# One-core decode block: 32 rows of the query weights by an indirect load in place of two side loads

## The chip, the core and the metric

The kernel runs on one core of one Trainium2 chip. The core has five engines that run their own instruction streams in order: PE (matrix products), DVE (vector), ACT (scalar), POOL (GpSimd) and SP (which here only starts transfers). Sixteen DMA engines move data between the chip's memory (HBM) and the on-chip memory of 128 partitions. The metric is device microseconds (us) of one execution; before the change three runs gave 138.19, 138.13 and 137.70 us, median 138.13 us.

## What is computed

A decode step of a transformer block, for four tokens (B = 4), all tensors in bf16:

```python
def _A_ref(x, k_cache, v_cache, wq, wo):          # attention over the last W = 2048 positions
    q = (x @ wq).reshape(B, 1, 32, 128).transpose(0, 2, 1, 3)
    k = jnp.repeat(k_cache[:, :, Sk - W:, :], rep, axis=1)     # 4 kv heads, rep = 8
    v = jnp.repeat(v_cache[:, :, Sk - W:, :], rep, axis=1)
    scores = jnp.einsum("bhqd,bhkd->bhqk", q, k) * (Dh ** -0.5)
    p = _softmax(scores, axis=-1)
    o = jnp.einsum("bhqk,bhkd->bhqd", p, v)
    return o.transpose(0, 2, 1, 3).reshape(B, 1, 4096) @ wo

def _B_ref(x, w1, w3, w2):                        # gated MLP, F = 3584
    h = _silu(x @ w1) * (x @ w3)
    return h @ w2

h = x + _A_ref(_layernorm(x), k_cache, v_cache, wq, wo)
h2 = h + _B_ref(_layernorm(h), w1, w3, w2)
```

Here x is 4 x 1024, wq 1024 x 4096, wo 4096 x 1024, w1 and w3 1024 x 3584, w2 3584 x 1024. With four tokens the arithmetic is small; 55.6 MB of weights and cache must be read.

## The kernel before

**The ring.** Every large operand is loaded by SP into one on-chip tile, `ring`, 81,920 bf16 columns wide on all 128 partitions (160 KiB each; `KIB` = 512 columns). `plan` (line 129) lists the loads in order with the column at which each lands, and `load_next` (line 149) issues the next entry wherever the code calls it. A region is used again once its earlier content has been read. With columns in brackets: wq rows 0 to 3 of each partition [0, 16384), wq rows 4 to 7 [16384, 32768), K of tokens 0 and 1 [32768, 49152), K of tokens 2 and 3 [49152, 65536), V of tokens 0 and 1 [65536, 81920), that is token 0 in [65536, 73728) and token 1 in [73728, 81920), V of tokens 2 and 3 [0, 16384), wo [16384, 49152), w1 [49152, 77824), w3 [0, 28672), and w2 in four pieces [28672, 57344).

**Who waits.** A framework tracks tiles in the order in which the program text names them: an instruction that reads columns waits for the last instruction named before it that writes them, and one that writes them waits for earlier readers and writers. Each load also waits for the landing of an earlier load whose semaphore it takes over. A planner then sets the order of each engine's instructions; each engine runs its own list strictly in order. SP's list decides when transfers start.

**Stages.**
- Layer norm of x, then `xn` is turned into `xnT` (line 196): partition p holds wq's input rows 8p to 8p + 7, row chunk kc = 8p + kc.
- The query product (lines 255 to 279): for each of 8 chunks kc, eight matmuls of 512 columns add into `q_ps`. Chunks 0 to 3 need the first wq load, chunks 4 to 7 the second.
- In chunk 7 the last 512 columns (`CE`) are not in the second load. They come in two side loads (`load_side`, line 115) into two `kT` buffers, on 20 and 12 partitions, four sets of rows each. Matching parts of `xn` are copied to `xs`, turned to `xsT` (lines 199 to 219), and eight matmuls (line 273) add the product.
- `q_sb`, `qt_ps`, `qz` (lines 280 to 290): the queries scaled, turned and spread.
- The K stage (lines 312 to 332): 16 units (token b, quarter n). Each has 16 PE transposes of K into two `kt_ps` buffers, a DVE copy and an ACT copy into a `kT` buffer, and, one unit later, four score matmuls that need `qz`. There are four `kt_ps` buffers and four `kT` buffers. wo's load is issued after unit 7.
- Softmax and its spreading `z` (lines 335 to 361), then 256 `OT_ps` matmuls with V (lines 380 to 390). w1's load is issued behind those of tokens 0 and 1, whose columns it overwrites.
- wo (lines 409 to 420; w3's and w2's first loads are issued in and behind it), the second layer norm up to `hnT`, w1 and w3 (`gate_up`), w2 (`down`), and the output.

`load_next(7)` at line 159 issues the first seven entries, up to V of tokens 0 and 1; line 271 issues V of tokens 2 and 3 behind chunk 3.

Of the kernel before, what the change touches and what calls it, by code (L numbers as in the profile page):

```python
# [10 lines left out]
P = 128  # L11
ACT = mybir.ActivationFunctionType
ALU = mybir.AluOpType
AX = mybir.AxisListType
BF16 = mybir.dt.bfloat16
FP32 = mybir.dt.float32


@with_exitstack
def kernel(  # L20
# [13 lines left out]
    nc = tc.nc  # L34

    B, _, D = A_x.shape
# [5 lines left out]
    KC = D // P  # L42
# [15 lines left out]
    ktpool = ctx.enter_context(tc.tile_pool(name="ktpool", bufs=4))  # L58
    wide = ctx.enter_context(tc.tile_pool(name="wide", bufs=2))
    const = ctx.enter_context(tc.tile_pool(name="const", bufs=1))  # L60
    act = ctx.enter_context(tc.tile_pool(name="act", bufs=1))
# [3 lines left out]
    JG = 4  # L65
    QD = P // JG
    RS = QD // B
    CQ = Hq * Dh // JG
# [11 lines left out]
    RING = 5 * 16384  # L80
# [8 lines left out]
    ring = stream.tile([P, RING], BF16)  # L89
# [19 lines left out]
    N_Q, N_F = Hq * Dh, F  # L109


    CE = 512
    SETS = [(0, 5, 4), (80, 3, 4)]

    def load_side(r0, ne, ns):

        t = ktpool.tile([P, JG * QD * 16], BF16, tag="kT")
        rows = A_wq[r0 * KC : (r0 + ne * 4 * ns) * KC, N_Q - CE : N_Q]
        rows = rows.rearrange("(t i k) n -> k i t n", i=ne, k=KC)[KC - 1]
        nc.sync.dma_start(out=t[: ne * 4, : ns * CE], in_=rows)  # L120
        return [t[: ne * 4, k * CE : (k + 1) * CE] for k in range(ns)]

    def load_tail(at, src, n, r0, m):

        t = ring[:, at : at + m * n]
        nc.sync.dma_start(out=t[:, : m * n - CE], in_=src[:, r0 * n : (r0 + m) * n - CE])
        return [t[:, k * n : (k + 1) * n] for k in range(m)]
    KIB = 512
    plan = [
        ("wq", load_rows, (0, wq_v, N_Q, 0, 4)),  # L130
        ("side", load_side, SETS[0]),
        ("side", load_side, SETS[1]),
        ("wq", load_tail, (32 * KIB, wq_v, N_Q, 4, 4)),
        ("k", load_kv, (64 * KIB, A_k_cache, 0)),
        ("k", load_kv, (96 * KIB, A_k_cache, 2)),
# [10 lines left out]
    loaded = {}  # L146
    cursor = [0]

    def load_next(n=1):
        for _ in range(n):  # L150
            if cursor[0] < len(plan):
                kind, f, args = plan[cursor[0]]
                loaded.setdefault(kind, []).extend(f(*args))
                cursor[0] += 1

    x_sb = act.tile([B, D], BF16)
    for c in range(2):
        nc.scalar.dma_start(out=x_sb[:, c * 512 : (c + 1) * 512], in_=x_flat[:, c * 512 : (c + 1) * 512])
    load_next(7)

    ident = const.tile([P, P], BF16)
    make_identity(nc, ident[:])
    eps_t = const.tile([P, 1], FP32)
    nc.vector.memset(eps_t[:], eps)

# [2 lines left out]
    for c in range(2):  # L168
        nc.sync.dma_start(
            out=x_q[c * 2 * QD : (c + 1) * 2 * QD : RS, :],  # L170
            in_=x_flat.rearrange("b (j c) -> j b c", j=JG)[2 * c : 2 * c + 2],
        )

    psA_cm = tc.tile_pool(name="psA", bufs=1, space=bass.MemoryType.PSUM)
    psA = psA_cm.__enter__()


    stats = act.tile([B, 2, nc.vector.BN_STATS_DIM], FP32)
    for c in range(2):
        nc.vector.bn_stats(out=stats[:, c, :], in_=x_sb[:, c * 512 : (c + 1) * 512])  # L180
    mv = act.tile([B, nc.vector.BN_AGGR_DIM], FP32)
    nc.vector.bn_aggr(out=mv[:], in_=stats[:])
    rstd = act.tile([B, 1], FP32)
    nc.scalar.activation(out=rstd[:], in_=mv[:, 1:2], func=ACT.Sqrt, bias=eps_t[:B], scale=1.0)
    nc.vector.reciprocal(out=rstd[:], in_=rstd[:])
    xn = act.tile([B, D], BF16)
    nc.vector.tensor_scalar(  # L187
        out=xn[:], in0=x_sb[:], scalar1=mv[:, 0:1], scalar2=rstd[:, 0:1],
        op0=ALU.subtract, op1=ALU.mult,
# [5 lines left out]
    xnT = act.tile([P, KC, B], BF16)  # L195
    nc.vector.tensor_copy(out=xnT[:], in_=tp_ps[:])


    NS = sum(ns for _, _, ns in SETS)
    ts_ps = psA.tile([P, NS, B], BF16, tag="kt1")  # L200
    xs = wide.tile([B, NS, 20], BF16, tag="w4k")
    sl = []
    for r0, ne, ns in SETS:
        v = xn[:, r0 * KC : (r0 + ne * 4 * ns) * KC]
        v = v.rearrange("b (s l i k) -> b k l i s", s=4, l=ns, i=ne)
        nc.vector.tensor_copy(
            out=xs[:, len(sl) : len(sl) + ns, : ne * 4].rearrange("b l (i s) -> b l i s", s=4),
            in_=v[:, KC - 1, :, :, :],
        )
        for l in range(ns):  # L210
            nc.tensor.transpose(
                out=ts_ps[: ne * 4, len(sl), :], in_=xs[:, len(sl), : ne * 4], identity=ident[:B, :B]
            )
            sl.append(ne * 4)
    xsT = act.tile([20, NS, B], BF16)
    k0 = 0
    for _, ne, ns in SETS:
        nc.vector.tensor_copy(out=xsT[: ne * 4, k0 : k0 + ns, :], in_=ts_ps[: ne * 4, k0 : k0 + ns, :])
        k0 += ns


    q_ps = psA.tile([P, CQ], FP32, tag="scores")
    nc.vector.memset(q_ps[:], 0.0)

    qz = act.tile([P, B, Hkv * QD + REP], BF16)
    nc.vector.memset(qz[:], 0.0)
    ident_f = const.tile([P, P], FP32)
    nc.vector.tensor_copy(out=ident_f[:], in_=ident[:])
# [3 lines left out]
        out=perm[:].rearrange("p (h dq) -> p h dq", dq=JG),  # L232
        in_=ident[:].rearrange("p (dq h) -> p h dq", dq=JG),
# [12 lines left out]
    for j in range(2, JG):  # L246
        nc.vector.tensor_tensor(
            out=same[:, 0, :], in0=same[:, 0, :], in1=ident[:, j * QD : (j + 1) * QD], op=ALU.add
# [3 lines left out]
        nc.vector.tensor_copy(out=same[:, j, :], in_=same[:, 0, :])  # L252


    for kc in range(KC):
        wq_t = loaded["wq"][kc]
        for hf in range(CQ // 512):
            for g in range(JG):
                c0 = g * CQ + hf * 512
                n = min(512, N_Q - CE - c0) if kc == KC - 1 else 512  # L260
                if n <= 0:
                    continue
                nc.tensor.matmul(  # L263
                    q_ps[QD * g : QD * g + B, hf * 512 : hf * 512 + n],
                    lhsT=xnT[:, kc, :],
                    rhs=wq_t[:, c0 : c0 + n],
                    start=(kc == 0),
                    stop=(kc == KC - 1 or (kc == KC - 2 and c0 + 512 == N_Q)),
                )
        if kc == RQ - 1:  # L270
            load_next()
            for k, np_ in enumerate(sl):
                nc.tensor.matmul(
                    q_ps[QD * (JG - 1) : QD * (JG - 1) + B, CQ - CE : CQ],
                    lhsT=xsT[:np_, k, :],
                    rhs=loaded["side"][k],
                    start=False,
                    stop=False,
                )
    q_sb = act.tile([P, CQ], BF16)  # L280
    nc.vector.tensor_single_scalar(out=q_sb[:, :512], in_=q_ps[:, :512], scalar=qscale, op=ALU.mult)
    nc.scalar.mul(out=q_sb[:, 512:], in_=q_ps[:, 512:], mul=qscale)
# [1 line left out]
    for r in range(REP):  # L284
        nc.tensor.transpose(out=qt_ps[:, r, :], in_=q_sb[:, r * Dh : (r + 1) * Dh], identity=ident[:])
    nc.vector.tensor_copy(
        out=qz[:, :, : Hkv * QD].rearrange("p b (g z) -> p b g z", g=Hkv)[:, :, :, :REP],
        in_=qt_ps[:].rearrange("p r (g x) -> p x g r", g=Hkv)[:, :B, :, :],
# [24 lines left out]
    for u, (b, n) in enumerate(units):  # L313
        k_v = loaded["k"][b]
        kT = ktpool.tile([P, NJ, P], BF16, tag="kT")
        for t in range(NJ // TB):
            kt_ps = psA.tile([P, TB, P], BF16, tag=f"kt{nt % 4}")
            for jj in range(TB):
                nc.tensor.transpose(  # L319
                    out=kt_ps[:, jj, :], in_=k_v[:, n * NJ + t * TB + jj, :], identity=ident[:]  # L320
# [21 lines left out]
        out=Pm[:], in_=scores_ps[:], func=ACT.Exp, bias=nmax[:], scale=1.0, accum_out=rsum[:]  # L342
# [6 lines left out]
    for c in range(NSB):  # L349
# [4 lines left out]
        for g in range(Hkv):  # L354
            if g % 2 == 0:
                nc.vector.tensor_scalar(  # L356
                    out=z[:, :, g, :], in0=pt_ps[:], scalar1=mask[:, g : g + 1], scalar2=None, op0=ALU.mult
# [10 lines left out]
        out=Dm[:], in0=ident[:].rearrange("p (g b r) -> p b g r", g=Hkv, b=B),  # L368
        scalar1=rinv[:, 0:1], scalar2=None, op0=ALU.mult,
# [10 lines left out]
    for b in range(B):  # L380
        for j in range(JK):
            nc.tensor.matmul(  # L382
                OT_ps[:, b, :],
                lhsT=loaded["v"][b][:, j, :],
                rhs=PTz[j // NJ][:, (j % NJ) * B + b, :, :],
                start=(j == 0),
                stop=(j == JK - 1),
# [21 lines left out]
    for i in range(IO):  # L409
        for j in range(JG):  # L410
            nc.tensor.matmul(  # L411
                y_ps[QD * j : QD * (j + 1), :],
                lhsT=o4[:, i, :, :].rearrange("p b s -> p (b s)"),
                rhs=loaded["wo"][i][:, j * CG : (j + 1) * CG],
                start=(i == 0),
                stop=(i == IO - 1),
# [27 lines left out]
        out=hn[:], in0=h1[:], scalar1=tot[:, 0:1], scalar2=rstd2[:, 0:1],  # L444
        op0=ALU.subtract, op1=ALU.mult,
# [4 lines left out]
        out=hnT[:].rearrange("p k x -> p (k x)"), in_=hn[:].rearrange("q (c k) -> q k c", k=KC)  # L450
# [3 lines left out]
    def gate_up(kind, out_ps):  # L454
# [27 lines left out]
        out=hgT[:].rearrange("p i x -> p (i x)"),  # L482
        in_=hg[:].rearrange("q s c -> q (s c)").rearrange("q (c i) -> q i c", i=IF),
# [18 lines left out]
    for i in range(R1, IF):  # L502
        for c, t in enumerate((ya_ps, yb_ps)):
            down(i, HC, c * HC, t, start=(i == R1), stop=(i == IF - 1), skip_group_check=True)
        if i == R2 - 1:
            for c, t in enumerate((ya_ps, yb_ps)):
                nc.tensor.matmul(
                    t[:, :HC], lhsT=ident_f[:], rhs=h2[:, c * HC : (c + 1) * HC],
                    start=False, stop=False, skip_group_check=True,
# [36 lines left out]
```

## Time and profile before

| quantity | value |
|---|---|
| runs | 137.70 to 138.19 us, median 138.13 us |
| span of the profiled execution | 136.0 us |
| PE, DVE, ACT, POOL busy | 72.3, 43.9, 31.0, 1.7 us |
| data moved by DMA | 55.75 MB, mean 410 GB/s |
| mean granted TensorE clock | 0.720 of full |
| K stage with the scores: first `kt_ps` on the chain to last score matmul | 29.27 to 58.59 us |

The span runs from the first to the last instruction of one profiled execution; the 138.13 us of the runs is 2.1 us more, for what lies around the span. A transfer has two times: its issue on SP, and its landing, when an engine that waits for it goes on. An engine's line "waited for: total, times, longest" says what ended its idle time.

### The profile page before, as it was taken

Reading aid. Unit: us, or ns where it says so; the run is one execution under the profiler, and the core shown is the slowest. Engines: PE = TensorE matmul, PEld = TensorE weight load, DVE = VectorE, ACT = ScalarE, POOL = GpSimd, SP = SyncE. Lnnn points to the kernel's source line nnn. Section 1 sums busy time; section 2 is a strip of 40 time slices with the busy share of each in tenths; the row PEclk is TensorE's granted clock in tenths of the full one; section 3 lists DMA queues with packets and bytes.
Section 4 is the critical chain, followed back from the end, with each engine's and each line's share of the span. In section 5 each row is a group of like instructions: output and inputs, shape, how many; then the busy total and the mean of one; then the engine's idle time right before and its main releaser. Section 6 shows DMA issues by size and latency. Waiting matters only on the chain.

```text
span 136.0 us, 2436 instructions
## 1 busy us (share of the span) xinstructions
PE 72.3 (53%) x1096; PEld 46.1 (34%) x1096; DVE 43.9 (32%) x79; ACT 31.0 (23%) x36; POOL 1.7 (1%) x8
## 2 busy tenths in 40 slices
PE   0004920979898989810525916791097000970981
PEld 0002300268374756500014905570043000430870
DVE  5055000043344444470994001206200596026010
ACT  3000000015555555609294300000001400000000
POOL 5000000000000000000000000000000000000000
PEclk9999975557999999985555555568556855568568
DMA  5999999999999999999989999989989899999970
GB/s 155 464 463 406 412 420 414 429 424 439 424 439 424 424 443 426 410 552 453 463 347 463 463 410 405 477 354 494 439 371 494 371 472 401 399 420 407 424 298 5
DMA packets 2650, 55.75 MB, mean 410 GB/s; under 512 B 296, under 2 KB 464, under 8 KB 720
## 3 DMA queue, kind: packets, MB, share of 16 engines
q1 hardware_dynamic: 2604, 55.58, 95.6%
q8 instruction: 8, 0.13, 0.3%
q10 hardware_dynamic: 36, 0.02, 0.0%
q14 instruction: 2, 0.02, 0.0%
HBM read 55.59 MB, written 0.01 MB: 409 GB/s over the span
## 4 chain that ended last, share of the span: by engine, by line
DMA 54%; PE 25%; ACT 11%; DVE 5%; SPq 2%; issue 1%; ACTq 0%
DMA ring<-in_B_w_dram 38%; DMA ring<-in_A_wq_dram 15%; PE kt_ps L319 11%; ACT kT L325 5%; PE scores_ps L304 5%; ACT z L360 3%; PE q_ps L263 3%; DVE rmax L336 2%; ACT Pm L341 2%; PE OT_ps L382 2%; DVE pT L350 1%; SPq L120 1%; PE g_ps L459 1%; DVE z L356 1%; ACT L341 1%
## 5 line engine op out<-in xcount | busy, mean ns | idle before, releaser
L325 ACT COPY kT<-kt_ps 128x1024 bf16<-128x1024 bf16 x16 | 15.9, 1013 | 13.4 <-PE kt_ps L319 13.4
L319 PE MATMUL kt_ps<-ident,ring 128*128 128x128 bf16 x256 | 18.0, 232 | 0.0
L319 PEld LDWEIGHTS <-ring 128*128 128x128 bf16 x256 | 16.0, 105 | 4.9 <-issue 4.9
L323 DVE COPY kT<-kt_ps 128x1024 bf16<-128x1024 bf16 x16 | 11.1, 692 | 16.5 <-PE kt_ps L319 16.5
L459 PEld LDWEIGHTS <-hnT 128*32 128x32 bf16 x128 | 5.5, 143 | 21.8 <-issue 19.2
L382 PE MATMUL OT_ps<-z,ring 128*128 128x32 bf16 x256 | 7.5, 188 | 8.5 <-ACT z L360 5.0
L459 PE MATMUL u_ps<-ring,hnT 128*32 128x448 bf16 x64 | 6.0, 563 | 11.0 <-DMA ring<-in_B_w_dram 11.0
L304 PE MATMUL scores_ps<-kT,qz 128*32 128x512 bf16 x64 | 9.9, 609 | 2.9 <-ACT kT L325 2.9
L263 PE MATMUL q_ps<-ring,xnT 128*4 128x512 bf16 x63 | 6.7, 595 | 7.8 <-DMA ring<-in_A_wq_dram 7.8
L382 PEld LDWEIGHTS <-ring 128*128 128x128 bf16 x256 | 7.4, 104 | 9.2 <-issue 9.2
L459 PE MATMUL g_ps<-ring,hnT 128*32 128x448 bf16 x64 | 5.9, 558 | 4.9 <-DMA ring<-in_B_w_dram 4.9
L492 PEld LDWEIGHTS <-hgT 128*32 128x32 bf16 x156 | 4.9, 134 | 6.2 <-issue 5.7
L411 PE MATMUL y_ps<-ring,o 128*32 128x256 bf16 x128 | 5.9, 371 | 0.8 <-DVE o L398 0.8
L514 ACT CAST res<-yb_ps 128x128 bf16<-128x128 f32 x1 | 0.3, 266 | 26.1 <-PE yb_ps L492 26.1
L492 PE MATMUL y_ps<-ring,hgT 128*32 128x256 bf16 x68 | 3.8, 419 | 4.4 <-DMA ring<-in_B_w_dram 4.4
L360 ACT ACTIVATE z<-pt_ps,mask 128x512 bf16<-128x512 f32 x8 | 5.3, 687 | 3.5 <-DVE z L356 3.5
L352 PE MATMUL pt_ps<-pT,perm 128*128 128x512 bf16 x4 | 2.4, 607 | 6.8 <-DVE pT L350 6.8
L263 PEld LDWEIGHTS <-xnT 128*4 128x4 bf16 x63 | 2.0, 115 | 11.7 <-issue 11.6
L194 PE MATMUL tp_ps<-ident,xn 4*128 4x4 bf16 x8 | 0.7, 200 | 10.0 <-DVE xn L187 10.0
L356 DVE TENSOR_SCALAR z<-pt_ps,mask 128x512 bf16<-128x512 f32 x8 | 5.5, 741 | 1.2 <-ACT z L360 0.8
L473 DVE RECIPROCAL eg<-eg 128x896 f32<-128x896 f32 x1 | 5.8, 5753 | 0.0
L411 PEld LDWEIGHTS <-o 128*32 128x32 bf16 x128 | 4.4, 131 | 3.1 <-DVE o L398 1.9
(85 smaller groups left out, 50.1 us busy)
## 6 DMA issues: line engine op xcount, KB each, us to landing
ring<-in_B_w_dram SPq DMA_DIRECT2D x2, 7168.0 KB, 22.5
ring<-in_A_k_cache_dram SPq DMA_DIRECT2D x4, 2048.0 KB, 27.6
ring<-in_A_v_cache_dram SPq DMA_DIRECT2D x4, 2048.0 KB, 29.2
ring<-in_B_w_dram SPq DMA_DIRECT2D x1, 4352.0 KB
ring<-in_A_wq_dram SPq DMA_DIRECT2D x1, 4096.0 KB, 12.2
ring<-in_A_wq_dram SPq DMA_DIRECT2D x1, 3968.0 KB
ring<-in_B_w_dram SPq DMA_DIRECT2D x1, 1792.0 KB
ring<-in_B_w_dram SPq DMA_DIRECT2D x1, 768.0 KB
```

The costliest lines, as they stand in the source:

```text
L263: nc.tensor.matmul(q_ps[QD * g : QD * g + B, hf * 512 : hf * 512 + n], lhsT=xnT[:, kc, :], rhs=wq_t[:, c0 : c0 + n], start=(kc == 0), stop ...
L304: nc.tensor.matmul(scores_ps[QD * g : QD * (g + 1), n * 512 : (n + 1) * 512], lhsT=qz_v[:, z0 : z0 + QD], rhs=kT_v[:, g, :, :], start=(b = ...
L319: nc.tensor.transpose(out=kt_ps[:, jj, :], in_=k_v[:, n * NJ + t * TB + jj, :], identity=ident[:])
L323: nc.vector.tensor_copy(out=kT[:, t * TB : (t + 1) * TB, :], in_=kt_ps[:])
L325: nc.scalar.copy(out=kT[:, t * TB : (t + 1) * TB, :], in_=kt_ps[:])
L356: nc.vector.tensor_scalar(out=z[:, :, g, :], in0=pt_ps[:], scalar1=mask[:, g : g + 1], scalar2=None, op0=ALU.mult)
L360: nc.scalar.mul(out=z[:, :, g, :], in_=pt_ps[:], mul=mask[:, g : g + 1])
L382: nc.tensor.matmul(OT_ps[:, b, :], lhsT=loaded["v"][b][:, j, :], rhs=PTz[j // NJ][:, (j % NJ) * B + b, :, :], start=(j == 0), stop=(j == J ...
L411: nc.tensor.matmul(y_ps[QD * j : QD * (j + 1), :], lhsT=o4[:, i, :, :].rearrange("p b s -> p (b s)"), rhs=loaded["wo"][i][:, j * CG : (j + ...
L459: nc.tensor.matmul(out_ps[QD * j : QD * (j + 1), hf, :HF], lhsT=hnT[:, k, :], rhs=loaded[kind][k][:, c0 : c0 + HF], start=(k == 0), stop=( ...
L473: nc.vector.reciprocal(out=eg[:], in_=eg[:])
L492: nc.tensor.matmul(out_ps[QD * j : QD * (j + 1), :n], lhsT=hgT[:, i, :], rhs=loaded["w2"][i][:, j * CG + c0 : j * CG + c0 + n], **kw,)
```

## The change

Chunk 7's part of wq for partitions 96 to 127 (32 whole rows of 4096 columns) leaves the second wq load. That load becomes two: partitions 0 to 95 with four rows, partitions 96 to 127 with three. The 32 rows come by one indirect load from GpSimd into `xg`, the last 4096 columns of the ring [77824, 81920). It has one index for each of 128 partitions; 96 of them are out of bounds and skipped, and `LANES` says which partitions get a row. `xg` is zeroed first by a DVE memset. `sel`, a 0/1 matrix, is built on POOL from nine pieces of `ident`; one matmul with it gives the indices, and another moves the 32 partitions' `xn` to the places where their rows land (`xgT`). Eight matmuls with `xgT` and `xg` are added behind chunk 6, over the whole 4096 columns; chunk 7 then runs on 96 partitions. The side loads, their copies, transposes and matmuls go.

`load_next(7)` becomes `load_next(4)` (wq, wq's rest, both K entries), and one `load_next()` (V of tokens 0 and 1) stands behind the indirect load and ahead of the product with `xg` in the program text.

```diff
-    CE = 512
-    SETS = [(0, 5, 4), (80, 3, 4)]
-    def load_side(r0, ne, ns):
...
+    XP = 96
+    LANES = [(0, 5), (1, 5), (2, 5), (3, 2), (4, 5), (6, 1), (8, 1), (10, 3), (15, 5)]
     def load_tail(at, src, n, r0, m):
         t = ring[:, at : at + m * n]
-        nc.sync.dma_start(out=t[:, : m * n - CE], in_=src[:, r0 * n : (r0 + m) * n - CE])
+        nc.sync.dma_start(out=t[:XP, :], in_=src[:XP, r0 * n : (r0 + m) * n])
+        nc.sync.dma_start(out=t[XP:, : (m - 1) * n], in_=src[XP:, r0 * n : (r0 + m - 1) * n])
...
-        ("side", load_side, SETS[0]),
-        ("side", load_side, SETS[1]),
...
-    load_next(7)
+    load_next(4)
+
+    xg = ring[:, RING - N_Q :]
+    nc.vector.memset(xg, 0.0)
...
+    sel = wide.tile([P, P], BF16, tag="w4k")
+    nc.gpsimd.memset(sel[:], 0.0)
+    m0 = XP
+    for e, n in LANES:
+        nc.gpsimd.tensor_copy(out=sel[:, e * 8 : e * 8 + n], in_=ident[:, m0 : m0 + n])
+        m0 += n
+    pidx = const.tile([P, 1], I32)
+    nc.gpsimd.iota(pidx[:], pattern=[[0, 1]], base=0, channel_multiplier=1)
...
+    pv = const.tile([P, 2], BF16)
+    nc.vector.tensor_copy(out=pv[:, 0:1], in_=pidx[:])
+    nc.vector.memset(pv[:, 1:2], 1.0)
+    id_ps = psA.tile([P, 2], FP32, tag="kt3")
+    nc.tensor.matmul(id_ps[:], lhsT=sel[:], rhs=pv[:], start=True, stop=True)
...
+    nc.vector.tensor_tensor(out=idx[:], in0=idf[:, 0:1], in1=idf[:, 1:2], op=ALU.add)
+    nc.gpsimd.indirect_dma_start(
+        out=xg, out_offset=None, in_=A_wq,
+        in_offset=bass.IndirectOffsetOnAxis(ap=idx[:, :1], axis=0),
+        bounds_check=D - 1, oob_is_err=False,
+    )
+    load_next()
...
+    xg_ps = psA.tile([P, B], FP32, tag="kt2")
+    nc.tensor.matmul(xg_ps[:], lhsT=sel[:], rhs=xnT[:, KC - 1, :], start=True, stop=True)
+    xgT = act.tile([P, B], BF16)
+    nc.vector.tensor_copy(out=xgT[:], in_=xg_ps[:])
...
     for kc in range(KC):
         wq_t = loaded["wq"][kc]
...
+        k = XP if kc == KC - 1 else P
+        q_row(xnT[:k, kc, :], wq_t[:k], kc == 0, kc == KC - 1)
         if kc == RQ - 1:
             load_next()
-            for k, np_ in enumerate(sl):
-                nc.tensor.matmul(
...
+        if kc == KC - 2:
+            q_row(xgT[:], xg, False, False)
```

`q_row(lhsT, rhs, first, last)` is the old eight-matmul loop as a function.

More of the change, by code (lines that the diff above doesn't have):

```diff
@@ L16 @@
 FP32 = mybir.dt.float32
+I32 = mybir.dt.int32
 @with_exitstack
@@ L109 @@
     N_Q, N_F = Hq * Dh, F
-    CE = 512
-    SETS = [(0, 5, 4), (80, 3, 4)]
-    def load_side(r0, ne, ns):
[L117 to L121, printed above, removed]
+    XP = 96
+    LANES = [(0, 5), (1, 5), (2, 5), (3, 2), (4, 5), (6, 1), (8, 1), (10, 3), (15, 5)]
+    assert sum(n for _, n in LANES) == P - XP and max(n for _, n in LANES) <= P // 16
     def load_tail(at, src, n, r0, m):
         t = ring[:, at : at + m * n]
-        nc.sync.dma_start(out=t[:, : m * n - CE], in_=src[:, r0 * n : (r0 + m) * n - CE])
+        nc.sync.dma_start(out=t[:XP, :], in_=src[:XP, r0 * n : (r0 + m) * n])
+        nc.sync.dma_start(out=t[XP:, : (m - 1) * n], in_=src[XP:, r0 * n : (r0 + m - 1) * n])
         return [t[:, k * n : (k + 1) * n] for k in range(m)]
@@ L175 @@
     psA = psA_cm.__enter__()
+    pv = const.tile([P, 2], BF16)
[3 more added lines that the diff above has]
+    nc.tensor.matmul(id_ps[:], lhsT=sel[:], rhs=pv[:], start=True, stop=True)
+    idf = act.tile([P, 2], FP32)
+    nc.vector.tensor_scalar(
+        out=idf[:, 0:1], in0=id_ps[:, 0:1], scalar1=float(KC), scalar2=float(KC - 1 + 4 * D),
+        op0=ALU.mult, op1=ALU.add,
+    )
+    nc.vector.tensor_single_scalar(out=idf[:, 1:2], in_=id_ps[:, 1:2], scalar=-4.0 * D, op=ALU.mult)
+    idx = act.tile([P, 1], I32)
+    nc.vector.tensor_tensor(out=idx[:], in0=idf[:, 0:1], in1=idf[:, 1:2], op=ALU.add)
[3 more added lines that the diff above has]
+        bounds_check=D - 1, oob_is_err=False,
+    )
+    load_next()
     stats = act.tile([B, 2, nc.vector.BN_STATS_DIM], FP32)
@@ L196 @@
     nc.vector.tensor_copy(out=xnT[:], in_=tp_ps[:])
[L199 to L219, printed above, removed]
+    xg_ps = psA.tile([P, B], FP32, tag="kt2")
+    nc.tensor.matmul(xg_ps[:], lhsT=sel[:], rhs=xnT[:, KC - 1, :], start=True, stop=True)
+    xgT = act.tile([P, B], BF16)
+    nc.vector.tensor_copy(out=xgT[:], in_=xg_ps[:])
     q_ps = psA.tile([P, CQ], FP32, tag="scores")
@@ L252, with q_row @@
         nc.vector.tensor_copy(out=same[:, j, :], in_=same[:, 0, :])
-    for kc in range(KC):
-        wq_t = loaded["wq"][kc]
+    def q_row(lhsT, rhs, first, last):
         for hf in range(CQ // 512):
@@ L259 @@
                 c0 = g * CQ + hf * 512
-                n = min(512, N_Q - CE - c0) if kc == KC - 1 else 512
-                if n <= 0:
-                    continue
                 nc.tensor.matmul(
[L264 to L268, printed above, removed]
-                )
+                    q_ps[QD * g : QD * g + B, hf * 512 : (hf + 1) * 512],
+                    lhsT=lhsT, rhs=rhs[:, c0 : c0 + 512], start=first, stop=last,
+                )
+    for kc in range(KC):
+        wq_t = loaded["wq"][kc]
+        k = XP if kc == KC - 1 else P
+        q_row(xnT[:k, kc, :], wq_t[:k], kc == 0, kc == KC - 1)
         if kc == RQ - 1:
             load_next()
-            for k, np_ in enumerate(sl):
-                nc.tensor.matmul(
[L274 to L279, printed above, removed]
+        if kc == KC - 2:
+            q_row(xgT[:], xg, False, False)
     q_sb = act.tile([P, CQ], BF16)
```

## The prediction

> **What bounds the kernel now.** The page first, then the chain of waits in order of time, then SP's waits, because SP's list decides when transfers start.
>
> ```profile
> span 136.0 us, 2436 instructions
> ...
> PEclk9999975557999999985555555568556855568568
> DMA  5999999999999999999989999989989899999970
> ...
> q1 hardware_dynamic: 2604, 55.58, 95.6%
> ```
>
> From 1.1 us (SP's first issue, 0.73 + 0.38) to the last landing near 132.4 (the last w2 matmuls start at 132.39 in the timeline) the DMA engines hardly pause: 95.6% of 136.0 is 130.0 us of packets in some 131.3. So the kernel is bound by transfers, a better spread over the 16 engines can save 1.3 us at most, and every pause in the stream of loads is paid. Compute matters where it holds back an issue until the stream runs dry. The chain's large pieces:
>
> ```profile
> 3.03 20.59 DMA ring<-in_A_wq_dram
> 23.66 3.60 PE q_ps L263 x31
> 27.29 0.70 DVE q_sb L281
> ...
> 29.27 3.47 PE kt_ps L319 x33
> ...
> 57.94 0.65 PE scores_ps L304 x4
> 58.62 2.30 DVE rmax L336
> ...
> 74.79 1.46 PE OT_ps L382 x48
> 76.27 22.49 DMA ring<-in_B_w_dram
> 98.80 1.68 PE g_ps L459 x14
> 100.48 29.74 DMA ring<-in_B_w_dram
> ```
>
> The second wq load lands at 23.62; q, the K stage, softmax and V of tokens 0 and 1 run until 76.25; only then is w1 issued (76.27), which lands at 98.76. The reader should see that the middle, 23.66 to 76.27, is compute, though the DMA row shows nines there: K, V and wo are loading. SP's waits say when:
>
> ```profile
> SPq L94 <- PE OT_ps L382: 23.3, 1, 23.3
> SPq L94 <- DMA ring<-in_A_v_cache_dram: 9.7, 2, 4.9
> ...
> SPq L94 <- DMA ring<-in_A_wo_dram: 5.2, 1, 5.2
> ```
>
> SP waits in order: before issuing w1 it waited twice for V, then 23.3 us for `OT_ps`. So V of token 1 had landed by 76.27 - 23.3 = 53.0, V of token 0 4.9 earlier (48.1); the next two, at that pace, 57.9 and 62.8. Behind w1's issue (0.33) SP waited 5.2 for wo, which thus landed at 81.8. The slack of w1's issue is therefore about 5 us, and no more.
>
> **Parts that lie beside other work (taken at 0).** Removed: two side issues (1.81 us on SP at 1.17), behind which the second wq load was issued at 3.03; the first wq load keeps the queue until 12.94, so an earlier issue gains nothing. On PE eight `ts_ps` transposes (0.35) and eight side matmuls (1.89 at 16.01) go, in a PE that waits 5.76 us for wq afterwards; on DVE four small copies (0.34 and 0.23). Added on POOL: one memset (nearest row 0.21), an iota and nine tiny copies (between 0.10, a 128x1 memset, and 0.29, the affine select): 1.2 to 3.1 us beside the present work that ends at 2.3, so `sel` is ready by 3.5 to 5.5. On DVE the memset of 2048 words: 0.17 for 128 and 0.28 for 272 words extend to 1.6, 0.91 for 1024 in `q_ps` to 1.8; it hides in the 4.9 us that DVE waits for x_sb. The index chain is one matmul (0.20) and four DVE instructions of 0.15 to 0.18. Behind it in DVE's list stand the reciprocal and `xn`; `xnT` was ready at 10.84, wq at 12.94, so 2.1 us are free at once, and 5.8 more behind the 32 matmuls. Without that cover the whole would cost 1 to 3 us. The second wq load is now two issues (0.38 to 0.44 each), x_q's two issues move ahead of V in SP's list and may wait there for the wq loads: V of token 0 is then issued near 23.6 and not 13.5, but its turn in the stream comes only when K ends, about 43. Bytes are equal: 32 rows of 8 KB leave, 256 KB come.
>
> [...]
>
> **The indirect load.** No row shows one. From below: x_sb's small loads on ACT's queue, issued at 0.74, were waited for until 7.92, some 7 us. From above: a load that stands behind the backlog, the 29.2 us of V (issue to landing). With an issue at 6 to 10 us it lands at 13 to 39. Token 1's V waits for it before its issue, and needs that issue before the stream reaches it at 48.1. So it costs 0 at both ends; above 47 each us costs one.
>
> **The wait that is added.** V of tokens 0 and 1 is named ahead of the product with `xg`, and token 1's half [73728, 81920) contains `xg`'s columns [77824, 81920). So the eight matmuls with `xgT` wait for token 1's V to land, and read what it wrote; their time is that of any data, but the product takes V's rows in place of the 32 wq rows. In PE's list they carry a wait for that load's semaphore besides the indirect load's, and the planner put 72 K transposes ahead of them and chunk 7's eight matmuls behind. Behind these on PE stands everything: `qt_ps`, all scores, the other 184 transposes; DVE and ACT wait for `q_sb` in their lists; the four `kT` buffers fill and stop.
>
> The sum, step by step:
> - The product with `xg` starts at 53.0, not 23.66. V1's place in the stream is unchanged.
> - 16 matmuls at 3.60 / 31 = 0.116 (half clock): 1.9. `q_sb`, `qt_ps` as before (27.27 to 29.27): 2.0. The K stage resumes at 56.9.
> - Left in it: 184 of 256 transposes at 1.01 / 16 = 0.063, 11.6; 64 score matmuls at 0.55 / 4, 8.8; together 20.4 at full clock. Waits for copies: below, 1.0, the ACT copy that the first score needs (mean 1013 ns on the page); above, 2.5, the old ratio (four units took 43.90 to 50.92, 1.755 each, of which 1.56 is PE). I take 1.5, nearer the lower end, as much K is already copied.
> - Half clock at the start. This stage had a mean clock of 0.94 over 29.35 us:
>
> ```profile
> 29.27:58.62 29.35, 26.37 (x320) 18.00 (x318) 11.36 (x18) 15.90 (x16) 0.00 (x0) 0.94 1.01 430
> ```
>
> so (1 - 0.94) x 2 x 29.35 = 3.5 us of it ran at half, costing half of that, 1.7. That came after 5.6 us of q work; now PE has stood idle for some 20 us. Below: 1.7; above: twice that, 3.5; I take 2.6.
> - K stage's end: 56.9 + 20.4 + 1.5 + 2.6 = 81.4 (80.0 to 83.3) against 58.6: 22.8 late. Softmax and `OT_ps` have only PE, DVE and ACT work in them, so w1 is issued at 76.27 + 22.8 = 99.1.
>
> [...]
>
> **What is late next.** wo overwrites K of tokens 0 and 1 and waits for their transposes: 56 more, and 24 scores between them in PE's list: 3.5 + 3.3 + 1.5 + 2.6 = 10.9, so it is issued near 67.8. V ends at 62.8: the stream pauses about 6 us. wo then takes 8192 KB at w1's rate, 7168 KB in 98.76 - 81.8 = 17.0: 19.4, plus a start of 1 to 2.5, landing near 89, 10 us ahead of w1's issue; this pause therefore costs nothing, the second one, 89 to 99, contains it.
>
> w1 from a cold queue: at least 17.0 + 1.0; from the first wq load (4096 KB, 12.2 us to landing) 12.2 + 3072 KB at w1's rate, 7.3, is 19.5. I take 19.3: landing at 118.4, 19.6 after 98.8. `hnT`, which ends at 96.1 in the timeline and now at 96.1 + 22.8 = 118.9, is as late, and hides behind w3's 17 us. w3 waits for `y_ps` (SP had it by 81.8 + 6.9 = 88.7): 111.5, 7 us before w1 ends, so the stream runs on as before. Span 136.0 + 19.6 = 155.6; the runs lie 2.1 above their span: **157.7 us**.
>
> **Rivals.**
> - The query product waits for the indirect load alone (no wait for V). Then q is ready at 27.3 as now and what changes is 40 matmuls behind the second load in place of 31, at most 9 x 0.116 = 1.0 more if the stream felt it, and a better spread, at most 1.3 less: 136.8 to 139.2, say 138, not slower. For it: the bytes are equal and the rest hides. Against: the columns overlap and the order of the text. It decides if `q_sb` comes before 30 us. Chance 0.05.
> - The clock stays at half through the K stage, as in 58.62 to 98.80 (means 0.54 to 0.58, PE less busy): its PE work of 20.4 doubles; 2.6 of that is counted above and 1.5 of copy waits vanish beside it: +16, 174 us. Against: the page's row of clocks shows nines while transposes run. 0.05.
> - The indirect load lands after 47 (skipped indices dear, or its turn late): each us adds one; at 52, 163 us. Against: the bounds above. 0.04.
>
> **How the numbers follow.** Forecast, slow by V's wait with the sizes above: 0.86. Its range: the K stage 80.0 to 83.3 (-1.4, +1.9), w1's start 18.0 to 20 (-1.3, +0.7), 1 us on each side for V's landing: 154 to 161.5. It holds about 0.82 of all; the third rival's near part lies next to it, so the range stands as it is. About 0.5% (0.7 us) is what this kernel's measurement can tell from no change. Slower 0.95, same 0.03, faster 0.02, the last two from the first rival.
>
> **What would show it.** In the profile after: the chain goes through V's load into `q_ps` with `xgT` at about 53; `q_sb` idles until 55; PE nearly idle from 31 to 53; the DMA row has two gaps, near 63 to 69 and 89 to 100; w1 issued near 99. Wrong if `q_ps` with `xgT` starts before 30, if DMA shows no gaps, or if the stage from 57 on runs 30 us or more.

## The result and the profile after

The change made the kernel slower: 170.88 us (five runs, 170.52 to 171.21) against 138.04, a ratio of 1.2389 with the 95% interval [1.2368, 1.241]. The forecast was 157.7 us, 154 to 161.5: the direction was right, three fifths of the size were foreseen, 13 us were not. The profiled execution has a span of 168.9 us, 2.0 below the median of the runs.

The page of the kernel after, first the rows of 40 slices (a slice is now 4.2 us), then the queue of the indirect load (packets, MB, share) and what was read from HBM:

```profile
span 168.9 us, 2439 instructions
...
DMA  7999999899999999905799650069999999999970
GB/s 249 389 473 210 204 235 196 171 413 435 427 435 433 435 435 427 388 19 186 310 497 485 279 235 0 0 221 439 421 439 435 435 435 439 462 404 396 419 291 4
...
q0 software_dynamic: 144, 0.26, 0.8%
...
HBM read 56.38 MB, written 0.01 MB: 334 GB/s over the span
```

Two things are to be seen. In the GB/s row there are two gaps, from about 72 and from about 101 us; two were forecast, at 63 and 89, so both are there and some 10 us late. And there is a stretch that nobody had forecast: from the fourth to the eighth slice, 13 to 34 us, the stream moves 171 to 235 GB/s in place of 406 to 439, while the DMA row above it still shows eights and nines. The engines are busy, but the bytes come at half the rate. The last line has 0.79 MB more read from HBM than the 55.59 of before.

The chain of waits after, in order of time (start, length, what):

```profile
11.32 24.28 DMA ring<-in_A_wq_dram,idx
35.62 28.67 DMA ring<-in_A_v_cache_dram
...
64.34 1.90 PE q_ps L267 x13
66.26 0.70 DVE q_sb L281
...
92.10 0.65 PE scores_ps L304 x4
92.77 2.30 DVE rmax L336
...
109.02 1.46 PE OT_ps L382 x48
110.49 21.12 DMA ring<-in_B_w_dram
131.65 2.41 PE g_ps L459 x16
...
134.20 31.25 DMA ring<-in_B_w_dram
```

V's load now stands in the chain ahead of `q_ps`, as the forecast said, but its end is 64.3 and not 53.0. From there on the steps are the forecast's: product and turning until 68.6, K stage until 92.75, w1's issue at 110.49, the last 37.3 us as before. The K stage's row of windows (columns as below):

```profile
68.60:92.77 24.17, 22.39 (x248) 13.41 (x247) 8.30 (x12) 13.98 (x14) 0.00 (x0) 0.87 0.73 304
```

Where the 11 us before V's landing come from is said by a row of SP's waits and one of PE's timeline:

```profile
SPq L103 <- DMA ring<-in_A_wq_dram: 19.0, 2, 14.4
```

```profile
34.74 2.73 PE L267 MATMUL q_ps<-ring,xnT 128*4 128x512 bf16 x24 [17.48 <-DMA ring<-in_A_wq_dram]
```

SP's issue of V waits 19.0 us in two waits for the second wq load, now in two pieces, and PE's chunks 4 to 6 start at 34.74, where they started at 23.66 before. So the second wq load lands 11 us late, and K and V stand behind it in the stream. In time order (windows of 4 us; the columns are length, busy PE, PEld, DVE, ACT and POOL with counts, clock, DMA share and, last, GB/s), before and then after:

```profile
13.50:17.50 4.00, 4.00 (x39) 1.25 (x28) 0.00 (x0) 0.00 (x0) 0.00 (x0) 1.00 1.04 447
17.50:21.50 4.00, 0.39 (x2) 0.08 (x1) 0.00 (x0) 0.00 (x0) 0.00 (x0) 0.68 0.91 393
```

```profile
13.50:17.50 4.00, 3.44 (x32) 0.93 (x31) 0.00 (x0) 0.00 (x0) 0.00 (x0) 1.00 1.20 262
17.50:21.50 4.00, 0.00 (x0) 0.00 (x0) 0.00 (x0) 0.00 (x0) 0.00 (x0) 0.86 0.82 176
```

The same matrix is loaded at 262 and 176 GB/s in place of 447 and 393.

### The profile page after: what moved, and what is told of

Its sections match the earlier page's. It is cut to its first block, busy times and chain, and to the rows that moved or that the text cites. A ratio compares the mean times of both kernels' runs of the same rounds, so it can differ in the third digit from the quotient of the medians.

```text
span 168.9 us, 2439 instructions
## 1 busy us (share of the span) xinstructions
PE 72.0 (43%) x1091; PEld 45.2 (27%) x1091; DVE 45.1 (27%) x82; ACT 31.1 (18%) x36; POOL 4.3 (3%) x20
## 3 DMA queue, kind: packets, MB, share of 16 engines
HBM read 56.38 MB, written 0.01 MB: 334 GB/s over the span
## 4 chain that ended last, share of the span: by engine, by line
DMA 62%; PE 18%; ACT 6%; issue 6%; DVE 4%; POOL 1%; POOLq 0%; SPq 0%; ACTq 0%; DVEq 0%
DMA ring<-in_B_w_dram 31%; DMA ring<-in_A_v_cache_dram 17%; DMA ring<-in_A_wq_dram,idx 14%; PE kt_ps L319 8%; PE scores_ps L304 5%; ACT z L360 3%; PE g_ps L459 1%; DVE rmax L336 1%; ACT Pm L341 1%; PE OT_ps L382 1%; ACT kT L325 1%; PE q_ps L267 1%; DVE pT L350 1%; DVE z L356 1%; ACT L341 1%
## 5 line engine op out<-in xcount | busy, mean ns | idle before, releaser
L319 PE MATMUL kt_ps<-ident,ring 128*128 128x128 bf16 x256 | 20.4, 241 | 3.3 <-DMA ring<-in_A_k_cache_dram 2.9
L319 PEld LDWEIGHTS <-ring 128*128 128x128 bf16 x256 | 17.2, 109 | 10.8 <-issue 6.8
L267 PE MATMUL q_ps<-ring,xnT 128*4 128x512 bf16 (+1 forms) x64 | 7.2, 618 | 18.1 <-DMA ring<-in_A_wq_dram 18.1
L459 PE MATMUL u_ps<-ring,hnT 128*32 128x448 bf16 x64 | 5.6, 540 | 11.3 <-DMA ring<-in_B_w_dram 11.3
L382 PEld LDWEIGHTS <-ring 128*128 128x128 bf16 x256 | 7.2, 102 | 5.7 <-issue 5.6
L267 PE MATMUL q_ps<-ring,xgT 128*4 128x512 bf16 x8 | 1.0, 608 | 18.0 <-DMA ring<-in_A_v_cache_dram 18.0
L267 PEld LDWEIGHTS <-xnT 128*4 128x4 bf16 (+1 forms) x64 | 1.9, 116 | 22.7 <-DMA ring<-in_A_wq_dram 18.3
L281 DVE TENSOR_SCALAR q_sb<-q_ps 128x512 bf16<-128x512 f32 x1 | 0.7, 692 | 22.1 <-PE q_ps L267 22.1
L411 PE MATMUL y_ps<-ring,o 128*32 128x256 bf16 x128 | 5.1, 337 | 0.8 <-DVE o L398 0.8
```

Of the source, the lines that this page charges most:

```text
L267: nc.tensor.matmul(q_ps[QD * g : QD * g + B, hf * 512 : (hf + 1) * 512], lhsT=lhsT, rhs=rhs[:, c0 : c0 + 512], start=first, stop=last,)
L319: nc.tensor.transpose(out=kt_ps[:, jj, :], in_=k_v[:, n * NJ + t * TB + jj, :], identity=ident[:])
L382: nc.tensor.matmul(OT_ps[:, b, :], lhsT=loaded["v"][b][:, j, :], rhs=PTz[j // NJ][:, (j % NJ) * B + b, :, :], start=(j == 0), stop=(j == J ...
L411: nc.tensor.matmul(y_ps[QD * j : QD * (j + 1), :], lhsT=o4[:, i, :, :].rearrange("p b s -> p (b s)"), rhs=loaded["wo"][i][:, j * CG : (j + ...
L459: nc.tensor.matmul(out_ps[QD * j : QD * (j + 1), hf, :HF], lhsT=hnT[:, k, :], rhs=loaded[kind][k][:, c0 : c0 + HF], start=(k == 0), stop=( ...
```

## The experiments

Two costs had to be told apart: the wait for V, and whatever halved the stream. The indirect load was the obvious suspect for the second: the chain names it, and it was in flight from 11.3 to 35.6 us, just that stretch.

**e1: V's issues behind the product.**

```diff
-    load_next()
...
-        if kc == RQ - 1:
-            load_next()
         if kc == KC - 2:
             q_row(xgT[:], xg, False, False)
+            load_next(2)
```

> The indirect load is kept; both V entries are issued behind the product with xg in the program text, so that product waits for the indirect load alone and reads the 32 wq rows. Theory (two separate causes: the wait for V, some 21 us, and a stream slowed to some 200 GB/s while the indirect load runs, some 11 us): the second wq load still lands near 34.7, q follows at once, 148 to 151 us. Rival A (the indirect load alone is the cause, the wait for V is free): 171 us. Rival B (the wait for V alone, the slow stream costs nothing on the path): 138 to 139 us.

Measured: 149.26 us, ratio 1.0829 [1.081, 1.0847]. The wait for V is worth 170.88 - 149.26 = 21.6 us, and 11 us are left without it; rivals A and B both fall.

**e2 and e3: the rows by a plain load from SP**, issued behind the second wq load and ahead of K, with the wait for V (e2) and without it (e3).

```diff
+    nc.sync.dma_start(out=xg[: P - XP, :], in_=A_wq.rearrange("(p i) n -> p i n", i=KC)[XP:, KC - 1, :])
...
-    nc.gpsimd.indirect_dma_start(
```

> The wait for V is kept; the 32 rows come by one plain load from SP behind the second wq load, in place of the indirect load (as in the changed kernel the product then takes V's rows in place of these 32). Theory (two causes): the stream runs at some 420 GB/s again, V of token 1 lands near 53, 158 to 161 us. Rival A (indirect load alone): 138 to 139. Rival C (the stream is slowed by the second wq load's split into 96 and 32 partitions): 171, with about 200 GB/s between 13 and 34 us again.

Measured: 169.28 us, 1.2268 [1.2247, 1.2289]. My theory fell here. Without any indirect load the stream was as slow as with it; this is what rival C, the split, had for it. The indirect load in place of the plain one costs 170.88 - 169.28 = 1.6 us here.

> Both: V's issues behind the product and the rows by SP. Theory: nothing is left of either cost, 137 to 139.5 us, with the second wq load landing near 24. Rival C (the split): 148 to 151. A better or worse spread over the DMA engines than before may show as up to 1.3 us either way.

Measured: 147.95 us, 1.0726 [1.0708, 1.0744], rival C again. Its windows:

```profile
13.50:17.50 4.00, 3.26 (x32) 0.83 (x24) 0.00 (x0) 0.00 (x0) 0.00 (x0) 1.00 1.22 262
17.50:21.50 4.00, 0.00 (x0) 0.00 (x0) 0.00 (x0) 0.00 (x0) 0.00 (x0) 0.83 0.81 172
```

No POOL load is in this kernel, and the rates are those of the kernel after (262 and 176). The indirect load only happened to be there. Against the plain load it costs 149.26 - 147.95 = 1.3 us; the wait for V, e2 less e3, is 21.3, in agreement with e1.

**e4: the indirect load with 32 indices, none skipped** (on 32 partitions, otherwise as e1).

> As e1, but the indirect load has 32 indices on 32 partitions, none skipped: 2 entries for each DMA engine in place of 8. If the slow stream is a price for each entry, skipped or not, some 3/9 of 11 us is left (two entries and a completion for each engine against eight and one): 141 to 143 us. If the 96 skipped ones are what is dear: 138 to 139. If it is a fixed price of a load that POOL starts beside SP's stream: 148 to 151.

Measured: 148.29 us, 1.0763 [1.0745, 1.0781]. It lies in the interval of a "fixed price", but that reading is undone by e3: nearly all of it is the split. Against e3 the short indirect load costs 0.3 us, against e1 it saves 1.0. Its queue carries 48 packets (16 x 3) where e1's carries 144 (16 x 9).

**e5: the second wq load in one piece**, over 128 partitions; otherwise e3, without the load of the 32 rows and without the product with `xg`.

```diff
-        nc.sync.dma_start(out=t[:XP, :], in_=src[:XP, r0 * n : (r0 + m) * n])
-        nc.sync.dma_start(out=t[XP:, : (m - 1) * n], in_=src[XP:, r0 * n : (r0 + m - 1) * n])
+        nc.sync.dma_start(out=t[0:128, :], in_=src[0:128, r0 * n : (r0 + m) * n])
```

> The kernel of e3 with the second wq load as one load of 128 partitions and all four rows, no xg product and no load of the 32 rows. Theory (a load that reaches only some partitions runs at about half rate, 10 us in e3): the second wq load lands near 23.5, 137.5 to 139 us; against the before kernel's 137.9 this also shows what its side loads are worth. Rival D (the slow stream is not the partition split but something else that e3 keeps, such as the DVE memset of the ring or the work on POOL): 148.

Measured: 138.17 us, 1.0024 [1.0015, 1.0034]. Its windows:

```profile
13.50:17.50 4.00, 3.15 (x32) 0.91 (x25) 0.00 (x0) 0.00 (x0) 0.00 (x0) 1.00 1.00 434
17.50:21.50 4.00, 0.00 (x0) 0.00 (x0) 0.00 (x0) 0.00 (x0) 0.00 (x0) 0.90 0.91 393
```

The stream is back at 434 and 393 GB/s, and 147.95 - 138.17 = 9.8 us are gone. Up to 0.9 of them may be the eight matmuls with `xg` (the query product takes 4.47 us in e3's chain and 3.61 in e5's); e11 below undoes the split alone. What e3 and e5 share (the memset of the ring, POOL's work, the index chain) and the loss of the old side loads cost 138.17 - 137.80 = 0.4 us together.

**e6: the split by rows**, so that only row 7 goes to 96 partitions.

```diff
+        nc.sync.dma_start(out=t[:, : (m - 1) * n], in_=src[:, r0 * n : (r0 + m - 1) * n])
+        nc.sync.dma_start(out=t[:XP, (m - 1) * n :], in_=src[:XP, (r0 + m - 1) * n : (r0 + m) * n])
```

> The kernel of e3 with the second wq load split by rows: rows 4 to 6 on 128 partitions, row 7 on 96, the 32 rows on 32 by SP. Theory (half rate for bytes in loads of fewer partitions): 0.79 + 0.26 MB at some 210 GB/s in place of 420, 2.5 us more than e5: 140 to 141.5. Rival E (the price is for each such load, not for its bytes): two loads in place of three, 144 to 148.

Measured: 140.31 us, 1.0204 [1.0163, 1.0245]: 2.1 more than e5 where 2.5 were expected for 1.05 MB at half rate. Between e3 and e6 only the form of the split differs, and it is worth 7.6 us: two loads that don't reach all partitions remain of three, but 1.05 MB of 4.2. Here the price went by bytes, not by loads.

**e7 and e8: which partitions, or how many?** The same 4.2 MB of e5 in parts: 32 to 95, 0 to 31, 96 to 127 (e7); 0 to 63, 64 to 127 (e8).

> The kernel of e5 with the second wq load in three: partitions 32 to 95, then 0 to 31, then 96 to 127. [...] Rival F (how many partitions decides: every load under 128 at half): 4.2 MB at half, 10 us more: 147 to 149.

> The kernel of e5 with the second wq load in two: partitions 0 to 63, then 64 to 127. Theory (which partitions) and rival F (how many): both at half, 10 us more than e5: 147 to 149. Rival G (only a count that is no power of two, such as 96, is slow): as e5, 138 to 139.

Measured: e7 143.20 us, 1.0393 [1.0376, 1.0409]; e8 148.81 us, 1.0797 [1.0781, 1.0813]. The windows of e7, then of e8:

```profile
13.50:17.50 4.00, 3.09 (x32) 0.72 (x24) 0.00 (x0) 0.00 (x0) 0.00 (x0) 1.00 1.20 426
17.50:21.50 4.00, 0.00 (x0) 0.00 (x0) 0.00 (x0) 0.00 (x0) 0.00 (x0) 1.00 0.79 164
21.50:25.50 4.00, 0.00 (x0) 0.00 (x0) 0.00 (x0) 0.00 (x0) 0.00 (x0) 1.00 1.09 229
```

```profile
13.50:17.50 4.00, 3.58 (x32) 0.94 (x31) 0.00 (x0) 0.00 (x0) 0.00 (x0) 1.00 1.29 262
17.50:21.50 4.00, 0.00 (x0) 0.00 (x0) 0.00 (x0) 0.00 (x0) 0.00 (x0) 1.00 0.64 131
21.50:25.50 4.00, 0.00 (x0) 0.00 (x0) 0.00 (x0) 0.00 (x0) 0.00 (x0) 1.00 1.24 262
```

A load of 64 partitions ran at 426 GB/s when they were 32 to 95, and at 131 to 262 when they were 0 to 63 and then 64 to 127 (over the three windows, 218 on average). So here the number of partitions isn't what counts (rival F), nor a number that is no power of two (rival G). The time of a packet agrees. For 32 KB, one partition's four rows, the windows give, as DMA share x 16 engines x 32 KB / rate, 1.21 us in e5's two, 2.50 to 2.53 in e7's last two, 2.48 to 2.58 in e8's three and 2.44 to 2.47 in e3's two. The DMA row counts that time as busy, so it shows eights and nines at half the bytes. Why these halves are slow no run shows. That 0 to 63 and 64 to 127 would be at half by which partitions they are, as e8's theory has it, was the author's assumption: no run ahead of these two had shown it, and both agree with it, e7 5.0 us above e5 and e8 10.6. 96 partitions, 0 to 95, ran at 172 to 262 GB/s in e3; how that loss comes about wasn't tried. Nor was one rival: in the loads of e5, e7 and e8 the rows read from HBM change together with the partitions written, so an effect of the rows read isn't excluded.

**e10 and e9: the idea of the change without its two accidents.** e10 is e1 with e6's split by rows; e9 is e10 with all 128 indices in bounds (the unused rows meet zero weights).

> The kernel of e1 (indirect load, V's issues behind the product) with the second wq load split by rows as in e6. Theory (the three costs add): e6's 140.3 plus what the indirect load costs beside a plain one, e1 less e3, 1.3 us, so 141 to 142.5. [...] If the indirect load hides here: 140 to 140.6.

> The kernel of e10 with all 128 indices in bounds: the 96 places that were skipped fetch row 8q + 7 of their own partition q and meet zero weights. If a skipped index is still read in full (e1 reads 56.38 MB from HBM, e3 and e4 55.59; 96 x 8 KB is 0.79), the time is e10's within 0.7 us and HBM reads are the same 56.38 MB, with 0.79 MB more moved. If skipping saves the transfer: some 1.8 us more than e10 (0.79 MB at 430 GB/s).

Measured: e10 141.29 us, 1.025 [1.0233, 1.0268]; e9 141.74 us, 1.0282 [1.0264, 1.0299]. The indirect load in place of e6's plain one costs 1.0 us here, against 1.3 in e1; a better spread over the engines, if there is one, doesn't pay for it. The pages of e10 and of e9:

```profile
q0 software_dynamic: 144, 0.26, 0.6%
...
HBM read 56.38 MB, written 0.01 MB: 404 GB/s over the span
```

```profile
q0 software_dynamic: 144, 1.05, 2.0%
...
HBM read 56.38 MB, written 0.01 MB: 403 GB/s over the span
```

HBM reads are equal, though only e9 delivers the 96 rows: a skipped index saved the delivery (0.26 MB against 1.05), not the read (with 32 indices and none skipped, e4, 55.59 MB are read). Its difference in time, 0.45 us, is at the edge of what the two intervals separate.

**e11: the changed kernel with the split alone undone**, which is the kernel that the forecast had reckoned with.

> The changed kernel with one thing undone: the second wq load is one load of 128 partitions and four rows (0.26 MB more; its last 32 rows are not used, and the product with xg takes V's rows as in the changed kernel). This is what the forecast reckoned with, 157.7 us plus 0.6 for the bytes. Theory (costs add, 170.9 less e3's 147.95 over e5's 138.17, 9.8): 160 to 162. If V's wait and the slow stream overlap in part: above 163.

Measured: 160.51 us, 1.1662 [1.1638, 1.1687], as expected from adding. Its chain:

```profile
25.93 28.12 DMA ring<-in_A_v_cache_dram
54.10 1.91 PE q_ps L266 x16
...
81.58 0.65 PE scores_ps L303 x4
...
99.97 20.87 DMA ring<-in_B_w_dram
```

V at 54.05 (forecast 53.0), wo's issue at 68.08 (67.8), K stage's end at 82.23 (81.4), w1's issue at 99.97 (99.1), its landing at 120.84 (118.4), span 158.2 (155.6). By an estimate 0.6 of the later V is the 0.26 MB that this kernel loads twice (at 430 GB/s).

No version here beats the kernel before; e5, the plainest, is 0.24% slower. In the kernel after, in e2 and in e11 the product with `xg` reads V's rows and not the 32 wq rows, as the prediction says: they show what the wait costs, not a kernel that one would keep.

## Why the prediction was right in kind and wrong in size

- **The wait that is added: right.** The product with `xg` waited for V of token 1, which overwrites those columns. Undone alone it gives back 21.6 us (e1), and 21.3 without the indirect load (e2 less e3). The forecast had 19.6; the 2.0 that are missing are about the size of what w1's load took beyond its term, below.
- **The failed step: "Bytes are equal: 32 rows of 8 KB leave, 256 KB come", and from it "V1's place in the stream is unchanged".** The split of the second wq load was priced as issues on SP, 0.38 to 0.44 us each, and taken at 0. Bytes were equal, the rate was not: with the split V of token 1 landed at 64.3, without it at 54.05. The split costs 10.4 us in the kernel after (170.88 - 160.51) and at most 9.8 without the wait (e3 less e5). The row that should have raised doubt was missing: all large loads of the trace of before go to 128 partitions, so it had no price for any other. That called for a bound from above on the time of these 4 MB, and none was given.
- **The indirect load: inside its bounds, and not quite free.** It was issued at 11.3, later than the 6 to 10 assumed, because its index chain stood in DVE's list behind the norm's wait for x_sb; it landed at 35.6, between 13 and 39. In e11, without the split, it landed at 25.93. It costs 1.0 to 1.6 us against a plain load (e10 less e6, e1 less e3, the kernel after less e2), which the forecast had at 0.
- **The K stage: right, with two terms off against each other.** 24.1 us (68.63 to 92.75) where 24.5 were reckoned; softmax to w1's issue 17.7, as before. Its mean clock of 0.87 is 6.3 us at half clock, reckoned as in the prediction, which lose 3.1 where 2.6 was taken. If the 20.4 us of matmuls held, some 0.6 is left for the waits for copies, for which 1.5 was taken and 1.0 was the bound from below. That the sum fits so well is partly luck.
- **w1 from a cold queue: too small.** 21.1 us from issue to landing (20.9 in e11) for 19.3; the bound from above was 20. The bound from below, 18.0, held 1.0 us for the start, which no run shows; nor does one show the 1 at the lower end of wo's start of 1 to 2.5. wo took 23.5 us from issue to landing, where 20.4 to 21.9 were reckoned.
- **wo's pause was free, the second gap contains it: right.** wo was issued at 78.6 and landed at 102.1; w1 was issued 8.4 later, and until then the stream stood still.
- **The rivals.** That the product waits for the indirect load alone is e1's order, not the change's. The clock did not stay at half: 0.87 on average in the K stage, and 1.00 from 76 us to its end. The late indirect load didn't come to pass: 35.6 is well ahead of 47.

Of the 13.2 us that the forecast missed, 10.4 are the split; the other 2.8 (160.51 - 157.7) are in e11 too: w1's load 1.6, V 1.05, and the rest small. That the costs add was tested, not assumed: the wait is worth 21.6 and 21.3 us with and without the indirect load, the split 10.4 and at most 9.8 with and without the wait.

## What to carry to other kernels

When a load is cut, ask which partitions each piece reaches, not only how many bytes and issues there are: a piece of 64 partitions ran at full rate or at half by which partitions it held (426 GB/s in e7, 218 on average in e8), and cutting by rows rather than by partitions cost 2.1 us where the other cost 9.8 (both with the eight matmuls more). A busy DMA row is no sign of a fast stream (a share of 0.81 stood beside 172 GB/s in e3, 0.91 beside 393 in e5); read it beside the GB/s row. And where a buffer lends its columns to a second tile, the order of the program text decides who waits for whom: two calls moved were worth 21.6 us here.

## What was not expected of the hardware

- The rate of a load went with its partitions: 426 GB/s for 32 to 95 (e7), 131 to 262 for 0 to 63 and 64 to 127 (e8), 172 to 262 for 0 to 95 (e3), all with the DMA share at 0.64 or more.
- A skipped index of an indirect load still read as much from HBM as one that delivers: 56.38 MB with 96 of 128 skipped (e10) and with none of 128 skipped (e9), 55.59 with 32 indices (e4). The difference is 96 rows of 8 KB.
- A load from a cold queue: 7168 KB took 20.9 to 21.1 us from issue to landing, against 17.0 from the landing of the load ahead of it in the stream of before. The stream itself was hardly slow in that time: the core's DMA moved 428 GB/s from 110.49 to 131.60, 9.0 MB where w1 has 7.3, so part of the load behind it came in the same 21 us.
